# A Fourier mixing layer and a gated feed-forward: four stages through DRAM, rewritten as one pipeline on chip

## The chip, the cores and the metric

One core of a Trainium2 chip runs the whole program. The metric is the device time of one execution in microseconds (us), given as the median of the runs; lower is better. Engines are named as in the profile: PE is the matmul engine, DVE the vector engine, ACT the scalar (activation) engine, POOL the GpSimd engine, SP the engine whose queue issues most of the transfers. Within one session, runs of one kernel differ by about 0.4% at most. The sessions ran on several chips; in each of them the kernel before took 4183 to 4188 us (median). In the views, PEld is PE's loading of weights, a name that ends in q is the instruction queue of an engine, and a digit of the 40 slices is a busy share in tenths.

## The reference

```python
X = np.fft.fft(x, axis=1)            # x: (8, 3008, 256) float32, real
X = np.fft.fft(X, axis=2)
t = X.real.reshape(24064, 256)       # tokens
gate = np.maximum(t @ w_gate, 0.0)   # w_gate, w_val: (256, 1536)
val = t @ w_val
out = (gate * val) @ w_out           # w_out: (1536, 256)
```

Two facts matter. The input is real, so token k and token 3008 - k of a batch are the sum and the difference of the same cosine and sine parts. The transform over the 256 features is a fixed matrix, so it can be multiplied into w_gate and w_val once.

## The kernel before

The kernel has four stages, one after the other. Each ends in DRAM and the next reads it back: the feature transform (to Yr, Yi), the 47-point part of the sequence transform (to Tr, Ti), the 64-point part (to Zg), and the feed-forward. The parts that the argument touches:

```python
    WB = 2                                # 47-point stage
    for n1c in range(0, N1, WB):          # N1 = 64, N2 = 47
        twc, tws = gen_trig(...)          # twiddle tables, made on DVE
        for b in range(B):
            # ... views vr, vi of Yr, Yi: 47 partitions x 2 runs of 256
            nc.sync.dma_start(out=rr[:]..., in_=vr)
            nc.scalar.dma_start(out=ri[:]..., in_=vi)
            # ... 4 matmuls 47x512 into par, pai
            nc.vector.tensor_tensor(t1[:], par[:], twc[:], op=mybir.AluOpType.mult)
            # ... 5 more products and sums on DVE -> trs, tis
            nc.sync.dma_start(out=Tr[b, :, n1c:n1c + w, :], in_=trs[:]...)
            nc.scalar.dma_start(out=Ti[b, :, n1c:n1c + w, :], in_=tis[:]...)
    # ... 64-point stage, weights
    for col in range(NT):                 # feed-forward: 188 tiles of 128 tokens
        # ... 2 transposed loads zz <- Zg
        for fc in range(DF // 128):       # 12
            for kc in range(2):
                nc.tensor.matmul(pg[:], lhsT=wg[kc][:, fs:fs + 128], rhs=zt[kc][:], ...)   # 128x128
                nc.tensor.matmul(pv[:], lhsT=wv[kc][:, fs:fs + 128], rhs=zt[kc][:], ...)
            nc.scalar.activation(g[:], pg[:], mybir.ActivationFunctionType.Relu)
            nc.vector.tensor_tensor(h[:], g[:], pv[:], op=mybir.AluOpType.mult)
            nc.tensor.matmul(po[:], lhsT=h[:], rhs=wo[fc][:], ...)
```

## Time and profile before

| what | number | where it is read |
|---|---|---|
| time | 4184.26 us median of 3 runs | timing |
| 47-point stage | 315 to 2340 us, about 8 us for each of 256 pieces | first and last records of its lines |
| feed-forward | 2634 to 4185 us, 8.25 us for each of 188 tiles | the same |
| DMA engines in the 47-point stage | 7% busy | table of windows |

The page of the kernel before: busy time, the span in 40 slices (busy tenths, the granted PE clock, the DMA engines), and the chain of waits.

```profile
span 4185.5 us, 47249 instructions
PE 2051.7 (49%) x13816; PEld 1179.2 (28%) x13816; DVE 2189.1 (52%) x5539; ACT 558.6 (13%) x2331; POOL 34.1 (1%) x96
PE   5653222222222222222222376777777777777777
DVE  8984445455455454554555444444444444444444
PEclk9885555555555555555555555789888888888888
DMA  5660000000000000000000254100000000000000
DMA 62%; PE 28%; DVE 4%; issue 3%; ACT 1%; SPq 1%; DVEq 0%; ACTq 0%; POOL 0%; POOLq 0%
DMA Ti<-tis 46%; PE pg L246 11%; DMA zz<-Zg 11%; PE po L252 7%; PE pv L247 7%; DMA tr<-Tr 3%; DVE xtp L150 2%; ACT g L250 1%; PE pr L151 1%; PE pz L211 1%; DVE yis L156 1%; DMA ri<-Yi 1%; PE pz L212 1%; SPq L215 0%; DVE xb L143 0%
```

No engine is full. The chain is 62% DMA, and one write, `Ti<-tis`, is 46% of the span, while the DMA row of the same slices shows 0 tenths. The table of windows puts numbers on the two long stages (us, busy time of each engine with its instructions, clock, DMA share, GB/s):

```profile
core 0: us, PE busy (x) PEld busy (x) DVE busy (x) ACT busy (x) POOL busy (x), PEclk, DMA share, GB/s
400.00:2300.00 1900.00, 462.07 (x948) 119.99 (x949) 992.92 (x1725) 34.67 (x57) 16.17 (x48) 0.50 0.07 24
2750.00:4180.00 1430.00, 1086.51 (x10464) 835.57 (x10462) 660.57 (x2266) 477.29 (x2092) 0.00 (x0) 0.87 0.09 25
```

The largest groups of the feed-forward (count, busy us, mean ns, idle time before them and what ended it):

```profile
L251 DVE TENSOR_TENSOR h<-g,pv 128x128 bf16<-128x128 f32 x2256 | 632.7, 287 | 767.7 <-ACT g L250 442.0
L246 PE MATMUL pg<-zz,tg 128*128 128x128 bf16 x4512 | 725.5, 244 | 354.1 <-DMA zz<-Zg 302.2
L250 ACT ACTIVATE g<-pg 128x128 f32<-128x128 f32 x2256 | 515.2, 275 | 1356.7 <-PE pg L246 822.9
```

DVE and ACT work on 128 columns at a time, and wait longer than they work: a chain of small links.

### The profile page before, as it was taken

Reading aid. Unit: us, or ns where it says so; the run is one execution under the profiler, and the core shown is the slowest. Engines: PE = TensorE matmul, PEld = TensorE weight load, DVE = VectorE, ACT = ScalarE, POOL = GpSimd, SP = SyncE. Lnnn points to the kernel's source line nnn. Section 1 sums busy time; section 2 is a strip of 40 time slices with the busy share of each in tenths; the row PEclk is TensorE's granted clock in tenths of the full one; section 3 lists DMA queues with packets and bytes.
Section 4 is the critical chain, followed back from the end, with each engine's and each line's share of the span. In section 5 each row is a group of like instructions: output and inputs, shape, how many; then the busy total and the mean of one; then the engine's idle time right before and its main releaser. Section 6 shows DMA issues by size and latency. Waiting matters only on the chain.

```text
span 4185.5 us, 47249 instructions
## 1 busy us (share of the span) xinstructions
PE 2051.7 (49%) x13816; PEld 1179.2 (28%) x13816; DVE 2189.1 (52%) x5539; ACT 558.6 (13%) x2331; POOL 34.1 (1%) x96
## 2 busy tenths in 40 slices
PE   5653222222222222222222376777777777777777
PEld 2430000000000000000000011555555555655655
DVE  8984445455455454554555444444444444444444
ACT  0000000000000000000000000233333333333333
POOL 1000000000000000000000000000000000000000
PEclk9885555555555555555555555789888888888888
DMA  5660000000000000000000254100000000000000
GB/s 138 188 172 24 24 24 24 24 24 24 24 24 24 24 24 24 24 24 24 24 24 24 78 136 134 39 26 26 26 26 24 26 26 26 24 26 26 25 25 25
DMA packets 289798, 178.02 MB, mean 43 GB/s; under 512 B 82688, under 2 KB 289024, under 8 KB 289536
## 3 DMA queue, kind: packets, MB, share of 16 engines
q1 hardware_dynamic: 154304, 86.33, 7.5%
q10 hardware_dynamic: 132928, 86.30, 6.5%
q0 software_dynamic: 2304, 2.36, 0.4%
q8 instruction: 108, 1.77, 0.2%
q14 instruction: 154, 1.26, 0.1%
HBM read 78.64 MB, written 86.25 MB: 39 GB/s over the span
## 4 chain that ended last, share of the span: by engine, by line
DMA 62%; PE 28%; DVE 4%; issue 3%; ACT 1%; SPq 1%; DVEq 0%; ACTq 0%; POOL 0%; POOLq 0%
DMA Ti<-tis 46%; PE pg L246 11%; DMA zz<-Zg 11%; PE po L252 7%; PE pv L247 7%; DMA tr<-Tr 3%; DVE xtp L150 2%; ACT g L250 1%; PE pr L151 1%; PE pz L211 1%; DVE yis L156 1%; DMA ri<-Yi 1%; PE pz L212 1%; SPq L215 0%; DVE xb L143 0%
## 5 line engine op out<-in xcount | busy, mean ns | idle before, releaser
L251 DVE TENSOR_TENSOR h<-g,pv 128x128 bf16<-128x128 f32 x2256 | 632.7, 287 | 767.7 <-ACT g L250 442.0
L246 PE MATMUL pg<-zz,tg 128*128 128x128 bf16 x4512 | 725.5, 244 | 354.1 <-DMA zz<-Zg 302.2
L247 PE MATMUL pv<-zz,tv 128*128 128x128 bf16 x4512 | 746.7, 243 | 0.0
L252 PE MATMUL po<-t,h 128*128 128x256 bf16 x2256 | 707.0, 313 | 20.9
L181 PE MATMUL pai<-ri,W47c 47*47 47x512 bf16 x256 | 152.1, 594 | 1125.6 <-DVE t_5993 L190 26.1
L250 ACT ACTIVATE g<-pg 128x128 f32<-128x128 f32 x2256 | 515.2, 275 | 1356.7 <-PE pg L246 822.9
L247 PEld LDWEIGHTS <-tv 128*128 128x128 bf16 x4512 | 499.6, 111 | 372.1 <-issue 319.5
L246 PEld LDWEIGHTS <-tg 128*128 128x128 bf16 x4512 | 431.6, 112 | 79.9 <-issue 75.3
L179 PEld LDWEIGHTS <-W47c 47*47 47x47 bf16 x256 | 31.5, 123 | 1028.6 <-issue 711.5
L252 PEld LDWEIGHTS <-h 128*128 128x128 bf16 x2256 | 244.1, 108 | 195.0 <-DVE h L251 123.7
L179 PE MATMUL par<-rr,W47c 47*47 47x512 bf16 x256 | 158.6, 620 | 232.0 <-DMA rr<-Yr 231.5
L182 PE MATMUL pai<-rr,W47ns 47*47 47x512 bf16 x256 | 156.0, 609 | 159.2 <-DMA rr<-Yr 159.2
L181 PEld LDWEIGHTS <-W47c 47*47 47x47 bf16 x256 | 32.4, 127 | 649.8 <-DMA ri<-Yi 629.4
L214 DVE CAST zs<-pz 64x512 bf16<-64x512 f32 x192 | 128.8, 672 | 161.2 <-PE pz L212 126.5
L151 PE MATMUL pr<-cb,xtp 128*128 128x256 bf16 x376 | 128.5, 342 | 103.5 <-DVE xtp L150 103.5
L211 PE MATMUL pz<-tr,W64c 64*64 64x512 bf16 x192 | 119.4, 622 | 115.1 <-DMA tr<-Tr 78.4
L180 PE MATMUL par<-ri,W47ps 47*47 47x512 bf16 x256 | 160.7, 628 | 2.2 <-DMA ri<-Yi 2.2
L59 ACT ACTIVATE si<-mf 47x512 f32<-47x512 f32 (+3 forms) x37 | 21.5, 582 | 1040.7 <-issue 1026.6
L152 PE MATMUL pi<-sb,xtp 128*128 128x256 bf16 x376 | 129.6, 345 | 0.0
L212 PE MATMUL pz<-ti,W64ps 64*64 64x512 bf16 x192 | 119.3, 621 | 0.0
L148 PE MATMUL ptr<-ident,xb 128*128 128x128 bf16 x376 | 99.0, 264 | 18.0 <-DVE xb L143 18.0
L75 DVE TENSOR_SCALAR co<-co 47x512 f32<-47x512 f32 (+3 forms) x37 | 14.5, 392 | 170.9 <-ACT co L74 170.9
(1988 smaller groups left out, 1904.2 us busy)
## 6 DMA issues: line engine op xcount, KB each, us to landing
xt<-in_x_dram SPq DMA_DIRECT2D x188, 128.0 KB
Yr<-yrs ACTq DMA_DIRECT2D x188, 64.0 KB
Yi<-yis ACTq DMA_DIRECT2D x188, 64.0 KB
rr<-Yr SPq DMA_DIRECT2D x256, 47.0 KB
ri<-Yi ACTq DMA_DIRECT2D x256, 47.0 KB
Tr<-trs SPq DMA_DIRECT2D x256, 47.0 KB
Ti<-tis ACTq DMA_DIRECT2D x256, 47.0 KB
tr<-Tr SPq DMA_DIRECT2D x184, 64.0 KB
```

What stands on the lines that cost most here:

```text
L151: nc.tensor.matmul(pr[:], lhsT=xtp[:], rhs=C_Db[kc][:], start=(kc == 0), stop=(kc == 1))
L179: nc.tensor.matmul(par[:], lhsT=W47c[:N2, :N2], rhs=rr[:], start=True, stop=False)
L180: nc.tensor.matmul(par[:], lhsT=W47ps[:N2, :N2], rhs=ri[:], start=False, stop=True)
L181: nc.tensor.matmul(pai[:], lhsT=W47c[:N2, :N2], rhs=ri[:], start=True, stop=False)
L182: nc.tensor.matmul(pai[:], lhsT=W47ns[:N2, :N2], rhs=rr[:], start=False, stop=True)
L211: nc.tensor.matmul(pz[:], lhsT=W64c[:N1, :N1], rhs=tr[:], start=True, stop=False)
L212: nc.tensor.matmul(pz[:], lhsT=W64ps[:N1, :N1], rhs=ti[:], start=False, stop=True)
L246: nc.tensor.matmul(pg[:], lhsT=wg[kc][:, fs:fs + 128], rhs=zt[kc][:], start=(kc == 0), stop=(kc == 1))
L247: nc.tensor.matmul(pv[:], lhsT=wv[kc][:, fs:fs + 128], rhs=zt[kc][:], start=(kc == 0), stop=(kc == 1))
L250: nc.scalar.activation(g[:], pg[:], mybir.ActivationFunctionType.Relu)
L251: nc.vector.tensor_tensor(h[:], g[:], pv[:], op=mybir.AluOpType.mult)
L252: nc.tensor.matmul(po[:], lhsT=h[:], rhs=wo[fc][:], start=(fc == 0), stop=(fc == DF // 128 - 1))
```

## The change

The intent is to keep everything on chip but one small shuffle per batch, and to let PE work without a break.

- The sequence length is split as 94 x 32. The input is folded: rows s and 3008 - s, and features d and 256 - d, are added and subtracted, which halves what must be transformed.
- Stage 1, a shuffle through DRAM (0.75 MB each way) and stage 2 of batch b+1 run as extra pieces between the feed-forward steps of batch b.
- The feature transform is multiplied into the gate and value weights once, in fp32.
- Mirror tokens: when the sum for token k has been used, one more matmul with minus twice the sine weights turns the same bank (the accumulation buffer that matmuls write) into the sum for token 3008 - k.
- The gather `xh` fetches rows in reverse order by an index list.

```diff
+    def load_x(b):
+        for p0, n in ((0, 80), (80, 14)):
+            nc.sync.dma_start(out=xl[p0:p0 + n], in_=...)
+        nc.gpsimd.indirect_dma_start(out=xh[:]..., in_offset=...IndirectOffsetOnAxis(ap=ix[:, b:b + 1], axis=0))   # 94 rows of 16 KB
+    def fold(b, eng): ...               # six elementwise operations; DVE for batch 0, POOL for the others
+    def plus(b, blk, f):
+        for i, acc in enumerate((G, V)):
+            nc.tensor.matmul(acc[:], lhsT=wc[i][:, fs], rhs=pq[:, 0, :], start=True, stop=False)
+            nc.tensor.matmul(acc[:], lhsT=ws[i][:, fs], rhs=pq[:, 1, :], start=False, stop=True)
+        nc.scalar.activation(gs[:], G[:], ACTF.Relu)
+        nc.vector.tensor_tensor(h[:, 0, :], gs[:], V[:], op=ALU.mult)
+    def minus(b, blk, f):               # same G and V
+        for i, acc in enumerate((G, V)):
+            nc.tensor.matmul(acc[:], lhsT=wm[i][:, fs], rhs=pq[:, 1, :], start=False, stop=True, ...)
+        nc.scalar.activation(gs[:], G[:], ACTF.Relu)
+        nc.vector.tensor_tensor(<h, rows reversed>, gs, V, op=ALU.mult)
+    def out_piece(b, blk, f): ...       # eight 128x256 matmuls, of the step 12 earlier
+    for t in range(n + NF):             # n = 8 batches x 3 blocks x 12 = 288 steps
+        if 0 < t <= n:
+            minus(*steps[t - 1])
+        if t < n:
+            plus(*steps[t])
+        for fn in extra.get(t, ()):     # pieces of the next batch: stage 1 at steps 1 to 8, shuffle at 9, ...
+            fn()
+        if t >= NF:
+            out_piece(*steps[t - NF])
-    <the four stages of the kernel before, Yr, Yi, Tr, Ti, Zg and the transposed loads>
```

## The prediction

> **What bounds the kernel now.** It is four stages one after another (first and last records of each line): feature transform to 310 us, 47-point stage 315–2340, 64-point stage 2342–2634, gated feed-forward 2634–4185. The chain of waits is 62% DMA; the write Ti<-tis alone is 46%. In the middle (table of windows, 400–2000) the DMA engines are 7% busy, PE's clock is 0.50, and one (batch, column pair) takes about 8 us, 256 of them. So half the time is the landing time of small strided transfers through DRAM. The feed-forward takes 8.25 us per 128 tokens (188 tiles): 12 small links matmul, Relu (275 ns), product (287 ns), matmul, plus 1.4 us of PE waiting for each transposed load.
>
> **What changes.** The DRAM round trips Yr, Yi, Tr, Ti, Zg and the transposed loads go; one small shuffle per batch stays, overlapped with the feed-forward of the batch before. The feature transform goes into gate/value weights (24 fp32 matmuls once). Mirror tokens cost only one added matmul into each of G and V. Matmuls become 512 wide.
>
> **Steady step** (288 = 8 batches x 3 blocks x 12 features):
> - PE: six 512-wide and eight 256-wide matmuls, 5120 columns. At clock 1 the trace issues 128-wide ones every 55–60 ns and follows a 256-wide one after 0.11 us, with weight loads hidden; so about 2.17 us (estimate).
> - DVE: two products from PSUM (47x512 from PSUM: 0.67 us, 0.60 start to start), with copies about 1.4 us.
> - ACT: two 512-wide Relus (0.60 us from the 128-wide one plus 0.83 ns per column, Trainium skill, "ScalarE: Activation LUTs", What ACT_TABLE_LOAD costs; consistent with 47x512 Sin at 0.62), with copies about 1.3 us.
> - Loop through G/V banks: V-minus, G-plus, Relu, product, next V-minus, with hand-over gaps read as 0.15, 0.04, 0.05 us: about 2.15 us. PE and this loop are nearly equal, so some stalls: I take 2.3 us a step.
>
> **Sum.**
> - Set-up before the first step: about 70 us (x and weights, some 20 us of small DVE table work, fold of batch 0 about 13 us, 24 [...] matmuls about 22 us, shuffle about 10 us).
> - Fold of batch 1 on POOL: 12,000 elements at 2.6 cycles of 1.2 GHz (Trainium skill, "GPSIMD Engine Reference", 3.1; no run here shows it) is about 26 us; PE, in order, should stall about 17 us for it in step 1. Later folds have 26 steps (60 us) for load plus fold, and should hide.
> - 288 x 2.3 = 662 us; transforms of seven later batches on PE about 22 us.
> - Tail: 12 output-only pieces and the last store, about 15 us.
>
> Total about 790 us, 5.3 times faster. All of what is removed is critical: the DMA latency of the 47-point stage goes entirely.
>
> **What would show it.** PE over 85% busy between 100 us and the end, clock near 1.0; a page without Ti; the chain of waits mostly PE with ACT/DVE of the G/V loop; one PE gap of 10–25 us at step 1 released by POOL; step spacing 2.2–2.4 us; DVE and ACT 55–65%.
>
> **What would make it wrong.** POOL folds over about 40 us stall PE in every batch (each 10 us excess is 60 us in all). The loop slower than read (extra evacuations of ACT and DVE landing ahead of Relu or product): 0.2 us a step is 58 us. A clock below 1 would raise PE's 2.17 us; before, it falls to half only where PE idles. Set-up DMA slower than thought: 20–40 us. If the loop's stalls are fully hidden, about 745 us.
>
> Predicted 790 us, range 745 to 890; faster by over 2%: 0.99, within 2%: 0.005, slower: 0.005.

## The result, and the profile after

The changed kernel takes 822.25 us (median of 4 runs, 821.95 to 822.91), against 4183.58 us for the kernel before in the same rounds. The ratio is 0.1965 (95% interval 0.1963 to 0.1968), or 5.1 times faster.

The page of the changed kernel, the same lines as before:

```profile
span 820.7 us, 12157 instructions
PE 696.3 (85%) x4432; PEld 433.2 (53%) x4432; DVE 491.5 (60%) x767; ACT 406.4 (50%) x699; POOL 203.8 (25%) x66
PE   0007433859999999999999999999999999999997
DVE  6143121636776676667666766676666666666662
PEclk9999865979999999999999999999999999999999
DMA  9302510262137213621271226212711141111112
PE 74%; DVE 7%; DMA 6%; POOL 4%; another core or an unknown queue 3%; SPq 2%; ACT 2%; issue 1%; POOLq 0%; DVEq 0%
```

The chain is now PE's. Nearly all of PE's lost time lies in the first nine slices. The groups that answer to those of before:

```profile
L341 DVE TENSOR_TENSOR h<-gs,V 128x512 bf16<-128x512 f32 x288 | 198.1, 688 | 199.9 <-ACT gs L339 147.4
L359 PE MATMUL po<-wo,h 128*128 128x256 bf16 x2304 | 297.8, 273 | 0.0
L328 ACT ACTIVATE gs<-G 128x512 f32<-128x512 f32 x288 | 172.3, 598 | 30.2 <-PE G L326 13.6
L89 POOL TENSOR_TENSOR xc<-xl,xh 94x3840 f32<-94x3840 f32 x7 | 58.2, 8314 | 362.8 <-DMA xl<-in_x_dram 362.8
```

What PE waited for, in the timeline of PE alone (start, duration, instruction, idle time before it and who ended it):

```profile
65.32 0.59 PE L115 MATMUL ps_240<-eo,wz 94*96 94x129 bf16 x4 [65.32 <-DVE eo L97]
...
104.95 0.19 PE L135 MATMUL psr<-t_276,rot 128*128 128x12 bf16 x1 [12.69 <-DMA t_276<-Td]
...
108.58 0.63 PE L325 MATMUL G<-pq,wc_84 128*128 128x512 bf16 x1
...
136.84 0.59 PE L115 MATMUL ps_434<-eo,wz 94*96 94x129 bf16 x4 [24.40 <-POOL eo L97]
...
137.44 0.63 PE L336 MATMUL G<-pq,wm_88 128*128 128x512 bf16 x1
137.87 0.63 PE L336 MATMUL V<-pq,wm_89 128*128 128x512 bf16 x1
```

The first step starts at 108.6 us. Step 1 then waits 24.4 us for POOL's fold of batch 1, as foreseen in kind. After that wait PE starts its 512-wide matmuls 0.43 us apart for about 3.6 us, and 0.216 us apart later. This agrees with the Trainium skill, "TensorE: Matmul & The Clock Gate", Part 1, which states a half clock after an idle window and about 3.4 us of activity to leave it. From 180.6 to 805 us PE is busy for 99.8% of the time:

```profile
core 0: us, PE busy (x) PEld busy (x) DVE busy (x) ACT busy (x) POOL busy (x), PEclk, DMA share, GB/s
180.60:805.00 624.40, 623.01 (x4094) 392.93 (x4094) 424.20 (x639) 366.73 (x633) 166.97 (x41) 1.00 0.29 79
```

The steps' spacing shows two values. In steps that carry a piece of the next batch's transform it is mostly 2.39 us. In all others it is 2.21 to 2.22 us, and it is exactly that also in the steps before the first output matmul, where PE has less to do. There the timeline shows what sets it:

```profile
147.70 0.38 PE L336 MATMUL V<-pq,wm_89 128*128 128x512 bf16 x1 [0.35 <-DVE h L329]
147.92 0.38 PE L325 MATMUL G<-pq,wc_84 128*128 128x512 bf16 x1
148.13 0.38 PE L326 MATMUL G<-pq,ws_86 128*128 128x512 bf16 x1
...
148.55 0.60 ACT L328 ACTIVATE gs<-G 128x512 f32<-128x512 f32 x1 [0.56 <-PE G L326]
...
149.18 0.69 DVE L329 TENSOR_TENSOR h<-gs,V 128x512 bf16<-128x512 f32 x1 [0.30 <-PE ps_532 L111]
...
149.92 0.38 PE L336 MATMUL V<-pq,wm_89 128*128 128x512 bf16 x1 [0.35 <-DVE h L329]
```

This is the loop that the prediction named. The mirror matmul into V must wait for the product that reads V; the new G follows it on PE; the Relu follows G; the product follows the Relu; then the next mirror matmul may go. One turn takes 149.92 - 147.70 = 2.22 us. (The releaser printed for the product is a matmul that had ended earlier; what ended last is the Relu, at 149.15.)

### The profile page after: what moved, and what is told of

The parts are those of the page before. It is cut to its first block, busy times and chain, and to the rows that moved or that the text cites. A ratio compares the mean times of both kernels' runs of the same rounds, so it can differ in the third digit from the quotient of the medians.

```text
span 820.7 us, 12157 instructions
## 1 busy us (share of the span) xinstructions
PE 696.3 (85%) x4432; PEld 433.2 (53%) x4432; DVE 491.5 (60%) x767; ACT 406.4 (50%) x699; POOL 203.8 (25%) x66
## 4 chain that ended last, share of the span: by engine, by line
PE 74%; DVE 7%; DMA 6%; POOL 4%; another core or an unknown queue 3%; SPq 2%; ACT 2%; issue 1%; POOLq 0%; DVEq 0%
PE po L359 28%; PE V L336 9%; PE G L325 7%; PE G L326 7%; PE V L326 7%; PE V L325 7%; PE G L336 7%; DVE h L329 2%; DMA t_590<-Td 2%; SPq L73 2%; DMA xl<-in_x_dram 2%; ACT gs L339 1%; DMA Td<-t_433 1%; DMA Td<-t_239 1%
## 5 line engine op out<-in xcount | busy, mean ns | idle before, releaser
L341 DVE TENSOR_TENSOR h<-gs,V 128x512 bf16<-128x512 f32 x288 | 198.1, 688 | 199.9 <-ACT gs L339 147.4
L359 PE MATMUL po<-wo,h 128*128 128x256 bf16 x2304 | 297.8, 273 | 0.0
L339 ACT ACTIVATE gs<-G 128x512 f32<-128x512 f32 x288 | 172.2, 598 | 241.4 <-PE G L336 241.4
L329 DVE TENSOR_TENSOR h<-gs,V 128x512 bf16<-128x512 f32 x288 | 197.8, 687 | 10.9 <-ACT gs L328 5.7
L328 ACT ACTIVATE gs<-G 128x512 f32<-128x512 f32 x288 | 172.3, 598 | 30.2 <-PE G L326 13.6
L89 POOL TENSOR_TENSOR xc<-xl,xh 94x3840 f32<-94x3840 f32 x7 | 58.2, 8314 | 362.8 <-DMA xl<-in_x_dram 362.8
L336 PE MATMUL V<-pq,wm_89 128*128 128x512 bf16 x288 | 109.0, 379 | 5.0 <-DVE h L329 3.6
L336 PE MATMUL G<-pq,wm_88 128*128 128x512 bf16 x288 | 109.8, 381 | 1.0 <-ACT gs L328 0.8
L326 PE MATMUL V<-pq,ws_87 128*128 128x512 bf16 x288 | 109.8, 381 | 0.0
L325 PE MATMUL V<-pq,wc_85 128*128 128x512 bf16 x288 | 109.7, 381 | 0.0
L326 PE MATMUL G<-pq,ws_86 128*128 128x512 bf16 x288 | 109.6, 381 | 0.0
L325 PE MATMUL G<-pq,wc_84 128*128 128x512 bf16 x288 | 109.5, 380 | 0.0
L90 POOL TENSOR_TENSOR xl<-xl,xh 94x3840 f32<-94x3840 f32 x7 | 58.2, 8316 | 0.6
L325 PEld LDWEIGHTS <-wc_84 128*128 128x128 bf16 x288 | 27.8, 97 | 52.8 <-issue 42.0
L365 ACT COPY os<-po 128x512 f32<-128x512 f32 x48 | 28.1, 585 | 43.8 <-PE po L359 43.8
L326 PEld LDWEIGHTS <-ws_87 128*128 128x128 bf16 x288 | 28.2, 98 | 34.7 <-issue 0.8
L325 PEld LDWEIGHTS <-wc_85 128*128 128x128 bf16 x288 | 28.0, 97 | 34.8 <-issue 0.8
L326 PEld LDWEIGHTS <-ws_86 128*128 128x128 bf16 x288 | 27.8, 97 | 34.5 <-issue 0.6
L363 DVE COPY os<-po 128x512 f32<-128x512 f32 x48 | 33.2, 692 | 8.4 <-PE po L359 8.4
```

Source lines behind the costliest of these rows:

```text
L89: eng.tensor_tensor(xc[:], xl[:, 1:J - 1, :], rev, op=ALU.subtract)
L90: eng.tensor_tensor(xl[:, 1:J - 1, :], xl[:, 1:J - 1, :], rev, op=ALU.add)
L325: nc.tensor.matmul(acc[:], lhsT=wc[i][:, fs], rhs=pq[:, 0, :], start=True, stop=False)
L326: nc.tensor.matmul(acc[:], lhsT=ws[i][:, fs], rhs=pq[:, 1, :], start=False, stop=True)
L328: nc.scalar.activation(gs[:], G[:], ACTF.Relu)
L329: nc.vector.tensor_tensor(h[:, 0, :], gs[:], V[:], op=ALU.mult)
```

## The experiments

Two experiments each lift one limit of the kernel before, and leave the rest of it as it is. The others work on the changed kernel. Comparisons among changed kernels are of medians, since each was timed beside the kernel before.

### 1. The 47-partition transfers cut in two (kernel before)

```diff
-                nc.sync.dma_start(out=rr[:]..., in_=vr)                 # 47 partitions
+                for p0, n in ((0, 32), (32, 15)):
+                    nc.sync.dma_start(out=rr[p0:p0 + n]..., in_=<rows p0 to p0 + n>)
 (likewise ri, Tr, Ti)
```

> The kernel before with every 47-partition transfer of the 47-point stage cut into 32 and 15 partitions, nothing else. Theory (few engines): a 47-partition transfer runs on a single one of the 16 DMA engines (the Trainium skill, 'DMA: Bandwidth & Descriptors', 'Why a DMA increments its semaphore by 16 and not by 1', gives the largest k up to 16 that divides the partition count, which is 1 for 47; the trace shows the engines 7% busy in this stage, about 1 in 16). Then the stage falls from 2025 us to what DVE needs, 256 x 6 x 0.60 us plus tables, 1000 to 1200 us, and the total to 3150 to 3400 us. Rival (landing latency of small transfers, as my prediction worded it): each transfer still takes its fixed time, the stage stays within 10%, total over 4000 us.

Measured: 3203.92 us, correct. The stage's matmuls into `pai` now start between 311 and 1334 us instead of 315 and 2321. The table of windows in that stage:

```profile
400.00:1300.00 900.00, 416.52 (x876) 125.45 (x876) 899.21 (x1607) 33.81 (x54) 27.21 (x48) 0.50 0.19 47
```

DVE is busy for 899 of 900 us: the stage went from waiting for transfers to being DVE's. My prediction called the 46% "the landing time of small strided transfers". That is wrong in its mechanism. More and smaller transfers made the stage twice as fast, so they had not waited a fixed latency each. The packed trace also keeps the start and duration of every single DMA packet (the views of `prof` show only sums of them), and there the one engine can be seen: in the kernel before, from 400 to 2300 us, a packet is always in flight, and for 1711 of these 1900 us exactly one, at 24 GB/s. With the cut, from 400 to 1300 us, up to 16 are in flight (for moments more), and for 437 of the 900 us none. Of the 3361 us that the whole change saves, 980 us were to be had by this edit alone.

### 2. The feed-forward widened to 512 tokens (kernel before)

```diff
-        for col in range(NT):                    # 128 tokens, pg, pv, h, g of 128x128
+        for col in range(T // 512):              # 512 tokens, pg, pv, h, g of 128x512, four po banks
```

> The kernel before with its feed-forward alone widened from 128 to 512 tokens a matmul, same arithmetic, same transposed loads, no mirror trick. If the 128-wide links (matmul, Relu 275 ns, product 287 ns, matmul) and the wait at each tile bound that stage, it falls from 1549 us to between PE's own 735 us (estimate: 47 tiles x 12 x four 512-wide and four 256-wide matmuls, 1.30 us) and 1000 us; total 3370 to 3640 us. Rival (the 376 transposed loads, about 3 to 4 us each, pace the stage): it stays above 1200 us, total above 3830 us.

Measured: 3533.71 us, correct, 652 us less. The stage takes about 890 us instead of 1549, with PE busy for 787 us of it (the columns of the table of windows and of the groups, as above):

```profile
2640.00:3530.00 890.00, 786.59 (x4424) 407.98 (x4512) 445.86 (x752) 331.73 (x564) 0.00 (x0) 0.97 0.15 42
L249 PE MATMUL pg<-zz,tg 128*128 128x512 bf16 x1115 | 412.2, 386 | 96.7 <-ACT g L253 79.4
```

So neither the arithmetic nor the number of transposed loads held that stage: both are as before. Two things went together. The links are wider and fewer, and PE's wait at each tile shrank: before `pg` it had been idle for 354 us, of which 302 for the transposed loads, and is now idle for 97 us. The edit also gives these loads more buffers (three for each half of the features, of 512 tokens, where there were three of 128 tokens in all), so how the 652 us divide between the links and the wait for loads is not shown. The arithmetic of the mirror trick was not needed for this part of the gain.

What the other parts of the change are worth on the kernel before (the fold, the merged weights, the overlap of the stages) was not run one by one. These two edits save 980 and 652 of the 3361 us, and the rest is not taken apart.

### 3. The gather cut in two (changed kernel)

```diff
-        nc.gpsimd.indirect_dma_start(out=xh[:]..., in_offset=...(ap=ix[:, b:b + 1], axis=0))
+        for p0, n, t in ((0, 80, ix), (80, 14, ix2)):      # ix2: the last 14 indices, from partition 0
+            nc.gpsimd.indirect_dma_start(out=xh[p0:p0 + n]..., in_offset=...(ap=t[:n, b:b + 1], axis=0))
```

> The changed kernel with the indirect gather of 94 rows cut into 80 and 14 rows. Theory (the 94-row gather uses few of the 16 DMA engines, 1.5 MB in 37 us even when little else runs): the first gather lands before 25 us instead of 52, the first gate matmul is at 68 to 75 us instead of 108.6, the batch-1 stall on POOL shrinks to about 18 us, the 9.5 us stall for the second shuffle goes; total 760 to 775 us. Rival (the weights queued at the same time hold the gather up): the gather still lands after 40 us, total above 805 us.

Measured: 762.46 us, correct, 59.8 us less than the changed kernel. Transfers from issue to landing, first in the changed kernel and then with the gather cut (queue, count, KB, median us to landing):

```profile
t_276<-Td SPq DMA_DIRECT2D x1, 768.0 KB, 24.3
t_590<-Td SPq DMA_DIRECT2D x1, 768.0 KB, 16.6
...
t_3488<-Td SPq DMA_DIRECT2D x1, 768.0 KB, 5.5
...
xh<-in_x_dram,ix POOLq DMA_INDIRECT x8, 37.5
```

```profile
t<-Td SPq DMA_DIRECT2D x8, 768.0 KB, 5.4
xh<-in_x_dram,ix POOLq DMA_INDIRECT x16, 9.6
```

```profile
38.13 0.59 PE L116 MATMUL ps<-eo,wz 94*96 94x129 bf16 x4 [38.13 <-DVE eo L98]
...
70.04 0.38 PE L329 MATMUL G<-pq,ws 128*128 128x512 bf16 x1
...
88.55 0.59 PE L116 MATMUL ps<-eo,wz 94*96 94x129 bf16 x4 [15.43 <-POOL eo L98]
```

The first gather has landed by 21.5 us instead of 51.9, the first fold now follows the table work without a wait, the first step starts at about 70 us, and both waits for the shuffle go. The shuffle read of 0.75 MB took 24.3 and 16.6 us when a gather was in flight beside it, and 5.3 to 7.1 us when none was. So the slow gather cost twice: by itself, and by holding up what shared its engines. The rival, contention from the weights, is not the main cause, since the weights are still loaded at the same time. It has a share in the first gather alone: that one took 50.1 us against 34.8 to 40.1 for the later ones, and after the cut 18.4 us against about 10.

How many engines the 94-row gather used can be read from the single packets in the trace of the changed kernel. From 211 to 246.5 us, a gather with no shuffle beside it, its queue has exactly two packets in flight for 26.4 of the 32.3 us in which it has any. The shuffle read issued at 80.6 us shows the price. Of its 1536 packets of 512 bytes, 1345 had started by 86 us, which is 14 sixteenths. From 86 to 97 us it then got 33 packets through, one for each of the 33 packets of 16 KB of the gather, and the rest followed when the gather had ended. So two of 16 engines carried the gather, in turns with the shuffle. Two is also what 94 = 2 x 47 gives by the rule of the Trainium skill ("DMA: Bandwidth & Descriptors", "Why a DMA increments its semaphore by 16 and not by 1") that experiment 1 rests on, the largest number up to 16 that divides the count of rows.

### 4. Half of the output matmuls left out (wrong result)

```diff
+            if ff % 2 == 0:
                 nc.tensor.matmul(po[:, s % 2, :], lhsT=ht[b, blk, ff][...], rhs=wo[:, ff, :], ...)
```

> The changed kernel with every second output matmul left out (wrong result on purpose). If PE's own work sets the step (PE 99.8% busy between 200 and 700 us), each step loses four matmuls of 0.109 us, 0.44 us, and the total falls by about 120 us to about 700 us. If the loop through the G and V banks is as long as PE's step (2.215 us apart in the first steps, which have no output matmuls), steps can fall only from the mean 2.30 to about 2.22 us, 22 us in all and 5 us in the tail: total 790 to 800 us.

Measured: 796.51 us. Nearly all mirror matmuls into V are 2.21 to 2.22 us apart from the first batch to the last, with or without transform pieces:

```profile
304.18 0.38 PE L336 MATMUL V<-pq,wm 128*128 128x512 bf16 x1 [0.33 <-DVE h L329]
306.39 0.38 PE L336 MATMUL V<-pq,wm 128*128 128x512 bf16 x1 [0.33 <-DVE h L329]
```

Taking away 0.44 us of PE work a step returned 26 us, not 120. An engine that is 99.8% busy was not the only limit. This fits the warning in the Trainium skill, "Trainium Kernel Development and Optimization", Performance Expectations, that matmul busy time is a bad metric for how close a kernel is to roofline; the page's reason, that matmuls are pipelined, is not tested by this run.

### 5. The mirror tokens computed afresh

```diff
-            nc.tensor.matmul(acc[:], lhsT=wm[i][:, fs], rhs=pq[:, 1, :], start=False, stop=True, skip_group_check=True)
+            nc.tensor.matmul(acc[:], lhsT=wc[i][:, fs], rhs=pq[:, 0, :], start=True, stop=False)
+            nc.tensor.matmul(acc[:], lhsT=wm[i][:, fs], rhs=pq[:, 1, :], start=False, stop=True)
 (and wm scaled by -1 instead of -2)
```

> The changed kernel with the mirror tokens computed afresh (start of a new sum, cosine and negated sine weights) instead of accumulated onto the finished banks: eight 512-wide matmuls a step instead of six, result still correct. PE sum: 0.43 us more a step, 2.60 us where no transform piece runs, total plus 105 to 122 us, 925 to 945 us. If instead the loop alone counted, it gets one 512-wide matmul longer (0.216 us), plus about 45 to 62 us, 865 to 885 us.

Measured: 927.90 us, correct, 105.7 us more. The spacing between steps without a transform piece is 2.60 us. Adding 0.43 us of PE work a step costs 106 us of the 124 that 288 steps would make, while taking 0.44 us away (experiment 4) earns 26. Both follow from two limits of almost the same length, 2.17 and 2.22 us. The mirror trick is worth 106 us here.

### 6. A better set-up

On top of the split gather, the gate weights are transformed before stage 1 of batch 0, and batch 1's pieces come nine steps later. Two small things go with it and are left out of the cut below: the copies of the gate's sine weights move from DVE to ACT, and the second-stage pieces of batch 1 stand two steps apart instead of three.

```diff
+        fold_weight(0)                 # gate weights: PE was idle until 38 us
         for c in range(8):
             stage1(0, c, ...)
         ...
+        fold_weight(1)
+            d = 9 if b == 0 else 0     # stage 1 of batch 1 at steps 10 to 17
```

> A better set-up on top of the split gather: the gate weights are transformed on PE before stage 1 of batch 0 (their loads have landed by then), and the transforms of batch 1 start nine steps later, so that PE does not wait for the POOL fold. If the split-gather run's reading is right (first gate matmul at 69.6 us, one 15.4 us stall), the first gate matmul comes at 60 to 65 us, no stall over 3 us is left, and the total is 735 to 748 us. If the stalls only move to another wait, over 752 us.

Measured: 744.24 us, correct, within the range. The first gate matmul comes at 59.2 us, a little earlier than expected. One expectation missed: a wait of 6.0 us for POOL's fold is left, where I expected none over 3 us.

### 7. The order of PE's matmuls changed, half of the output matmuls (wrong result)

```diff
         if 0 < t <= n:
-            minus(*steps[t - 1])
-        if t < n:
-            plus(*steps[t])
+            minus_g(*steps[t - 1])
+        if t < n:
+            plus_g(*steps[t])          # new G before the old V
+        if 0 < t <= n:
+            minus_v(*steps[t - 1])
+        if t < n:
+            plus_v(*steps[t])
```

> The half-output kernel (wrong result on purpose) with PE's order changed: both G matmuls of the new step go ahead of the V matmul of the mirror tokens, so the new Relu no longer waits behind the old product. Theory (the loop V mirror, G new, Relu, product, V mirror of 2.215 us set that run's steps): the loop loses the Relu and two matmuls and is about 1.7 us (estimate from 0.216, 0.15, 0.60, 0.69 and 0.05 us), so the steps fall to 1.75 to 1.90 us and the total from 796 to 690 to 730 us. Rival (something else, such as DVE or ACT work or stores, held the steps at 2.2 us): total stays above 780 us.

Measured: 746.87 us, outside the range. The steps did what the theory said: plain ones are 1.82 us apart, ones with a transform piece mostly 1.95 us. So the loop is what held experiment 4 at 2.22 us. The total missed because a new wait appeared, in the list of PE's waits (us in total, times, longest):

```profile
PE ps L115 <- DVE eo L97: 65.3, 1, 65.3
PE psr L135 <- DMA t<-Td: 60.1, 7, 13.9
```

With shorter steps the shuffle of every next batch came too late, 60.1 us in all. The estimate of 1.7 us for the loop was also low: from the mirror matmul to the start of its product the trace shows 0.48 us, where I had taken 0.37.

### 8. The same with the split gather (wrong result)

> The half-output, reordered kernel (wrong result on purpose) with the split gather added. That kernel missed its range (746.9 us against 690 to 730) although its steps fell to 1.82 us as expected: PE then waited seven times for the second half of the shuffle, 60 us in all. If those waits come from the slow 94-row gather sharing DMA engines with the shuffle, they all go (60 us), and the set-up gains what it gained before (27 us for the first gather, 9 us less waiting for POOL): 640 to 665 us. If the shuffle itself is too slow for short steps, its waits stay and the total is over 690 us.

Measured: 641.15 us. The wait for the shuffle is gone from the list:

```profile
PE ps L116 <- DVE eo L98: 38.1, 1, 38.1
PE ps L116 <- POOL eo L98: 17.1, 1, 17.1
```

The change of order and the split gather together bring experiment 4's kernel from 796.5 to 641.2 us. That closes the miss of experiment 7.

### 9. The order alone, all work kept

> The changed kernel with only the new order of matmuls. PE keeps its 2.17 us step, so only the 0.045 us by which the loop exceeds it in about 170 steps and the first dozen steps gain: 808 to 815 us (1 to 2% faster). If the loop had cost more than the trace shows, below 800 us.

Measured: 811.29 us, correct, 11.0 us less than the changed kernel. As expected, little: PE's own 2.17 us lies just under the old loop.

### 10. Better set-up and new order

> The better set-up plus the new order of matmuls, all work kept, correct result. With the loop at about 1.7 us PE's 2.17 us is the only limit: steps without transform pieces fall from 2.215 to 2.17 us, the first twelve (no output matmuls) to below 1.9 us; 8 to 15 us less than the better set-up alone, 722 to 738 us.

Measured: 730.93 us, correct. Steps without a transform piece are 2.16 to 2.17 us apart, those before the first output matmul 1.82 us. The faster first steps exposed the POOL fold again:

```profile
PE ps L116 <- POOL eo L98: 10.4, 1, 10.4
```

### 11. Batch 1's pieces five steps later still

```diff
-            d = 9 if b == 0 else 0
+            d = 14 if b == 0 else 0    # stage 1 of batch 1 in steps 15 to 22, its stage 2 in steps 30 to 35, one a step
```

> The better set-up and new order, with the transforms of batch 1 five steps later still (stage 1 in steps 15 to 22), because the last run left one 10.4 us wait of PE for the POOL fold there. That wait goes: 718 to 723 us, correct. If the shuffle of batch 1 then comes too late for its first use, the wait reappears at the second stage and the total stays at 726 us or more.

Measured: 720.16 us (5 runs, 719.91 to 720.54), correct, ratio to the kernel before 0.1721 (95% interval 0.1719 to 0.1723). This beats both kernels: 102 us (12%) below the changed one. Its table of windows between set-up and tail:

```profile
90.00:700.00 610.00, 610.00 (x4099) 393.97 (x4097) 407.35 (x642) 343.35 (x636) 169.49 (x47) 1.00 0.36 88
```

With the loop at 1.82 us, PE's own work is now the limit that the step spacing shows.

## Why the prediction was right, point by point

The measured time, 822 us, lies in the range of 745 to 890 and is 4% above the 790 us of the text. The terms of the sum, with the change points read from the trace (the first step at 108.6 us, the last mirror matmul at 804.7, the end at 820.7; the sum of the text's terms is 786):

| term | predicted, us | measured, us | how measured |
|---|---|---|---|
| set-up before the first step | 70 | 108.6 | first gate matmul |
| waits of PE in batch 0's steps | 17 | 33.9 | 24.4 for POOL's fold and 9.5 for the second shuffle |
| 288 steps with transform pieces | 662 + 22 | 662 | 804.7 - 108.6 - 33.9 |
| tail | 15 | 16 | 820.7 - 804.7 |

- **The set-up was mis-sized by 39 us.** I assumed that the input would be there before the tables; the gather landed at 51.9 us, and the shuffle behind its successor cost another 12.7 us. Experiment 3 shows the cause: with the gather cut in two the first step starts at about 70 us, the predicted figure. The prediction had named this risk ("Set-up DMA slower than thought: 20–40 us") without its cause. The other terms of the set-up held: the fold of batch 0 took 13.4 us for 13, the 24 fp32 matmuls 21.8 us for 22 (0.43 us for each of two records a matmul, so four times the 0.216 us of a bf16 one).
- **The waits were mis-sized by 17 us.** The POOL fold took the 26 us foreseen, but started later, since the input of batch 1 came late. The figure behind it, 2.6 cycles of 1.2 GHz per element of a two-input operation (the Trainium skill, "GPSIMD Engine Reference", 3.1), agrees with the trace: 3840 elements took 8.31 us, 2.16 ns each (DVE: 4.15 us). The 9.5 us for the shuffle was not foreseen at all; it has the same cause, and goes with the split gather.
- **The steps were over-estimated by 22 us.** I took 2.3 us a step and added 22 us for the transform pieces. The trace shows 2.22 us without pieces, 2.39 with them, 2.30 on average with everything in it. The sum of PE's work (2.17 us) was exact to the resolution of the trace, as experiment 10 shows. The loop was read as 2.15 and is 2.22 us.
- **"PE and this loop are nearly equal"** is shown: taking PE work away returns 26 us instead of 120 (experiment 4), and changing the order then shortens the step (experiment 7).
- **"Later folds ... should hide"** is shown: after batch 1 the list of waits has no wait of PE for POOL.
- **"DVE and ACT 55–65%"** held for DVE (60%) and not for ACT (50%). "PE over 85% busy between 100 us and the end" held, at a clock near 1, and so did the spacing of 2.2 to 2.4 us and the one gap of 10 to 25 us at step 1, released by POOL.
- **"So half the time is the landing time of small strided transfers"** was wrong as a mechanism, and cost nothing here since all of it was removed. It was one DMA engine's throughput (experiment 1). The same blindness made me miss the slow gather in the new kernel: 94 rows kept two packets in flight, 47 rows one.

So the total was close partly because two errors had opposite signs: 56 us too little in the set-up and its waits, 22 us too much in the steps; to that extent its closeness is luck. What the prediction got right by reasoning is the steady state, which is four fifths of the time.

## What to carry to other kernels

Look at how many DMA engines a transfer uses before calling it latency: a small DMA share with a long chain of DMA waits, and a number of rows like 47 or 94 that no number near 16 divides, were the sign here, and cutting the rows (into 32 and 15, or 80 and 14) was a test of a few lines. When accumulation buffers are used again in place, add up the loop from matmul through ACT and DVE back to matmul, and compare it with PE's own work; where the two are close, neither the busy share nor the wait list told which one limits; the steps that have less PE work, and an experiment that takes work away, did. After shortening the steady step, look again at everything that had just been hidden behind it: here the shuffle (experiment 7) and the fold (experiment 10) came back at once.

## What the Trainium skill lacked or had wrong

- "TensorE: Matmul & The Clock Gate", Part 2, "Back-to-back issue gap", gives a sustained spacing of about 81 ns at 128 columns and 131 ns at 512 for streams of weight load and matmul, and calls the formula N/2.4 + 2.5 ns right only for isolated ones. Here every matmul of the steady step has its own weight load, and the spacing is the formula's: 0.21 to 0.22 us at 512 columns, and 55 to 60 ns at 128 in the kernel before.
- "DMA: Bandwidth & Descriptors", "Why a DMA increments its semaphore by 16 and not by 1", gives the rule for the number of engines and an exception for direct copies issued by POOL, but does not mention indirect ones. A 94-row gather had two packets in flight, as the general rule would have it, and landed after 37.5 us (median); the same data as 80 and 14 rows landed after 9.6 us.
- The same page, "Queues, rings and completion order", states that an engine takes turns between queues, but no page that I read warns of its price: a 0.75 MB read took 16.6 to 24.3 us beside such a gather and 5.3 to 7.1 us without, since on the shared engines it got one packet of 512 bytes for each of 16 KB.
- No page that I read treats a loop through accumulation buffers used again in place as a limit of its own; here it was 2.22 us against 2.17 us of PE work, and 1.82 us after a change of order.
